# Scores of two heads by one matmul: pooled keys spread into zero-padded pairs, in a kernel of attention and two mixtures of experts

## The chip, the cores and the metric

The kernel runs on one core of one Trainium2 chip. The metric is the device time of one execution in microseconds (us). An execution covers everything from the first load to the last store; several executions are timed, and one further execution is recorded by the hardware profiler.

## The reference

Three layers follow one another. Only the first is touched by the change.

```python
# layer 1: q, k, v are (4, 8, 576, 64) float32; B=4 sequences, H=8 heads, S=576, D=64
k_p = k.reshape(B, H, Sp, pool, D).mean(axis=3)      # pool = 8, so Sp = 72 pooled keys
v_p = v.reshape(B, H, Sp, pool, D).mean(axis=3)
scores = scale * np.matmul(q, k_p.transpose(0, 1, 3, 2))
attn = softmax(scores)
x = np.matmul(attn, v_p)                              # rows become (2304, 512)
# layer 2: (2304, 512) -> 1536 -> 512
gate = 1 / (1 + np.exp(-(x @ w_gate)))
x = gate * (x @ w_val) @ w_out
# layer 3: 8 experts, every token to all of them, weights P from 8 rounds of row/column scaling
out = sum(P[:, e:e+1] * (np.maximum(x @ w1[e], 0) @ w2[e]) for e in range(8))
```

## The kernel before, in words

The 2304 tokens are cut into six blocks (`j` = 0 to 5) of 384, each of three tiles (`t`) of 128 tokens. Precision is kept by splitting operands into a high and a low part and running three passes of matmuls (`mm`, L225, and `x2_step`, L549). Layer 3 comes last and takes from about 570 us to the end; it isn't touched.

Layers 1 and 2 run interleaved. Layer 2 is a list of 72 steps, one per block and per slice `f` of the hidden width: a gate product G and a value product V (12 matmuls of 384 columns each, both recorded at L225, tile `gv`) and an output product X (12 matmuls at L549, tile `big`). For the first 36 steps the blocks 0, 1 and 2 take turns, so that a slice's weights serve two blocks. A slice that is met for the first time is made from raw 64-bit words: a load, a scaling (L152 or L154), five VectorE operations (L161, L162, L171, L174, L177), a high part by ScalarE (L195) and a low part by VectorE (L199), which is the last thing the product waits for. The slice is then stored (`store_words`) and later loaded again (`load_words`). I number these made weights m0, m1, ... in the order G, V, X of slice 0, then of slice 1 and so on; m10 is the V weight of slice 3, used in step 5.

Attention for a block is a chain of small pieces. `load_q` brings a tile with 64 x 2 partitions: partitions 0 to 63 hold the even heads, 64 to 127 the odd ones. `pool_k` sums groups of eight keys on VectorE into `kp` in the same two halves. `scores` (L341) fills a PSUM bank for one tile and one half `g`: four matmuls, each with 64 rows (one head's 64 dimensions), 128 weight columns (tokens) and 72 moving columns (pooled keys). A float32 matmul appears in the trace as two instructions, so a group of `scores` is 8. Then `maxima` (VectorE, L366 and L367), `exps` (ScalarE, L373, blocks 0 to 2) or `softmax` (blocks 3 to 5), `divide`, `turn` (TensorE transposes, L402), `keep_a` (ScalarE copy, L407), `values` (L416), `x_high` (ScalarE, L428) and `x_low` (VectorE, L432). For the first two sequences the values are pooled by TensorE (`spread_v`, L319, five pieces) and kept by ScalarE (`keep_v`, L328); otherwise by `pool_v` on VectorE.

The order in which every engine gets its work is set when the program is built. `Plan.run` takes tasks with keys (due times), costs and needs (`room`: free buffers), and hands each engine the first task by key whose needs are met by its own clock. On the chip every engine then executes its list strictly in that order, and each instruction waits for its semaphores. SyncE issues all the loads and stores of this part in one list. The table `FETCH` gives the keys of the first loads; `LEAD`, `START` and `V_LATE` say how far ahead of its block attention is planned. From step 60 on, the order is written out in plain code.

Of the kernel before, what the change touches and what calls it, by code (L numbers as in the profile page):

```python
# [10 lines left out]
F32 = mybir.dt.float32  # L11
# [10 lines left out]
def attention_moe_moe_kernel(  # L22
# [217 lines left out]
    class Attention:  # L240

        def __init__(self, at, spread):
            self.at, self.spread = at, spread
            for name in ("kp", "vp", "qs", "krs", "vrs", "es", "dens", "turned", "mx", "pt"):
                setattr(self, name, {})
# [25 lines left out]
        def pool_k(self, b, hp):  # L271
            if b not in self.kp:
                self.kp[b] = self.at.tile([128, HP, SP], F32, tag="kp", name="kp", bufs=2)
            nc.vector.tensor_reduce(
                out=self.kp[b][:, hp],
                in_=self.krs.pop((b, hp)).rearrange("p (s j) -> p s j", j=POOL),
                axis=AX.X,
                op=ALU.add,
            )

        def spread_k(self, b, c, tag):
            if c == 0:
                self.pt["k", b] = bank(*tag)
                self.kp[b] = self.at.tile([128, HP, SP], F32, tag="kp", name="kp", bufs=2)
            pt = self.pt["k", b][:, : HP * SP].rearrange("p (i s) -> p i s", i=HP)
# [49 lines left out]
        def scores(self, j, t, g, tag):  # L335
            pt = bank(*tag)
            sc = self.pt["s", j, t, g] = pt[:, 0 : 4 * SP].rearrange("p (h s) -> p h s", h=4)
            pr = slice(64 * g, 64 * g + 64)
# [70 lines left out]
        def values(self, j, t, tag):  # L409
# [410 lines left out]
    with tc.manual_schedule():  # L820
# [8 lines left out]
        for base_, step_ in ((512, -8), (-505, 8)):  # L829
# [11 lines left out]
            {  # L841
                "at": 2, "big": 4, "gv": 2, "wide": NWIDE, "made": NMADE, "wa": NWA, "kr": 4, "vr": 4,
                "q": 4, "e": 2, "a": 2, "xs": 3, "h": 3, "g": 2, "kp": 2, "vp": 2,
            }
# [29 lines left out]
        def took():  # L874
# [7 lines left out]
            ("k", 0): -39.0,  # L882
            ("q", 0): -38.5,
            ("v", 0): -25.0,
            ("w", 1): -21.0,
            ("w", 2): -17.0,
            ("k", 1): -8.5,
            ("q", 1): -7.5,
            ("v", 1): -6.5,
        }  # L890
        OFF = {"g": 0.0, "v": 0.5, "o": 1.0}
        wide_of = {}
# [30 lines left out]
        def pool(b, key, step):  # L923
# [20 lines left out]
            else:  # L944
                ks = [
                    add(FETCH.get(("k", b), key - 3) + 0.01 * i, "SP", 0.45, partial(A.load_k, b, i), room=[("kr", 1)], size=0.295, step=step)
                    for i in range(HP)
                ]
                pk = [
                    add(  # L950
                        key + 0.01 * i, "DVE", 0.72, partial(A.pool_k, b, i), [ks[i]],
                        room=[("kp", 1)] if i == 0 else None, frees=[("kr", 1)], step=step,
                    )
                    for i in range(HP)
                ]
            key += V_LATE
# [20 lines left out]
            else:  # L977
                vs = [
                    add(FETCH.get(("v", b), key - 3) + 0.01 * i, "SP", 0.55, partial(A.load_v, b, i), room=[("vr", 1)], size=0.295, step=step)
                    for i in range(4)  # L980
                ]
                pvs = [
                    add(
                        key + 0.01 * i, "DVE", 1.2, partial(A.pool_v, b, i), [vs[i]],
                        room=[("vp", 1)] if i == 0 else None, frees=[("vr", 1)], step=step,
                    )
                    for i in range(4)
                ]
            pooled[b] = pk, pvs

        V_LATE = 4.3
        START = -5.5
        LEAD = {0: 30.0, 1: 28.0, 2: 9.0, 3: 27.0, 4: 14.0, 5: 20.0}
        ends_in = [((b + 1) * S - 1) // TB for b in range(B)]

        def attend(j):
# [4 lines left out]
            if j == 1:  # L1001
                lo, lead = START, n - 1.0 - START
            step = lo - 1
# [10 lines left out]
            ms = []  # L1014
            es = []
            for t in range(TPB):
                qt = add(FETCH.get(("q", j), at_key(0.0) - 2) + 0.1 * t, "SP", 0.45, partial(A.load_q, j, t), room=[("q", 1)], size=0.262, step=step)
                for g in range(2):
                    key = at_key(0.1 + 0.12 * t + 0.06 * g)
                    s = add(  # L1020
                        key, "PE", (1.0, 0.55), with_bank(("s", j, t, g), partial(A.scores, j, t, g)), kps + [qt],
                        cond=free_tag, frees=[("q", 1)] if g else (), step=step,
                    )
                    first = (t, g) == (0, 0)
                    m = add(
                        key, "DVE", 0.93 if j >= DIRECT else 0.6, partial(A.maxima, j, t, g), [s],
                        room=[("e", 1)] if first else None, frees=gives(("s", j, t, g)) if j >= DIRECT else (), step=step,
                    )
                    ms.append(m)
                    if j < DIRECT:  # L1030
                        es.append(add(key, "ACT", 1.2, partial(A.exps, j, t, g), [m], table="exp",
                            frees=gives(("s", j, t, g))
                            + [("kp", 1) for b in range(B) if ends_in[b] == j and (t, g) == (TPB - 1, 1)]))
            if j >= DIRECT:
                x = add(
                    at_key(0.48), "ACT", 1.65, partial(A.softmax, j), ms, step=step, table="exp",
                    frees=[("kp", 1) for b in range(B) if ends_in[b] == j],
                )
            for t in range(TPB):
# [6 lines left out]
                for g in range(2):  # L1046
# [6 lines left out]
                        add(  # L1053
                            key, "ACT", 0.58, partial(A.keep_a, j, t, g), [r],
                            room=[("a", 1)] if g == 0 else None, frees=gives(("a", j, t, g)), step=step,
# [3 lines left out]
                vv = add(  # L1059
                    key, "PE", (1.25, 0.9), with_bank(("x", j, t), partial(A.values, j, t)), cs + vps,  # L1060
                    cond=free_tag, step=step,
                    frees=[("a", 1)] + [("vp", 1) for b in range(B) if ends_in[b] == j and t == TPB - 1],
                )
                xh = add(key, "ACT", 0.6, partial(A.x_high, j, t), [vv], room=[("xs", 1)] if t == 0 else None, step=step)
                xl = add(key, "DVE", 0.69, partial(A.x_low, j, t), [xh], frees=gives(("x", j, t)), step=step)
# [727 lines left out]
```

## Time and profile before

| | us |
|---|---|
| executions timed | 2051.07, 2058.88, 2059.80 (median 2058.88) |
| the profiled execution | 2051.49 |
| its span, first to last instruction | 2049.8 |
| first score matmul | 7.58 |
| first product of layer 2 | 43.41 |

The profile lists, for each engine, busy time and the groups of instructions, and for each stretch of the span what the engines did. PE is TensorE's matmuls, PEld its weight loads, DVE is VectorE, ACT ScalarE, POOL GpSimd, SP SyncE. A matmul's duration includes the time in the pipeline, so what one costs is read from the distance between starts, not from its duration. The granted clock of TensorE is given per stretch; before its first record the profile prints 1.00.

### The profile page before, as it was taken

The numbers are of one execution on the slowest core, as the hardware profiler recorded it, in microseconds if no ns is written. First come the engines' busy times: TensorE is split into PE (matmuls) and PEld (weight loads), VectorE is DVE, ScalarE is ACT, GpSimd is POOL, SyncE is SP. The second block draws the span as 40 slices with busy tenths as digits, with TensorE's granted clock in tenths as the row PEclk, the third lists the DMA queues.
The fourth block names the chain that finished last, engine by engine and source line by source line (L and its number), as shares of the span: only waits on it lengthen the run. The fifth ranks groups of instructions, "written<-read, shape, count | busy, mean of one in ns | idle before, by whom it ended". The sixth has DMA issues, their size and how long they took to land.

```text
span 2049.8 us, 33256 instructions
## 1 busy us (share of the span) xinstructions
PE 2021.3 (99%) x12721; PEld 1930.4 (94%) x12721; DVE 1257.1 (61%) x2302; ACT 786.3 (38%) x1611; POOL 682.5 (33%) x629
## 2 busy tenths in 40 slices
PE   8999999999989999999998999999999999999998
PEld 5999999999979888898888999999999999999998
DVE  7888754332168776666664656656565665656555
ACT  6734322322144443433334444444443333333332
POOL 0000000001144654445425566556654222222222
PEclk9999999999999999999999999999999999999999
DMA  7587588588866777667778877887789767676764
GB/s 262 202 313 278 185 296 302 193 299 288 322 244 233 282 277 257 247 244 264 257 270 327 295 279 279 291 284 269 279 284 372 274 248 251 240 257 227 263 241 159
DMA packets 171854, 544.83 MB, mean 266 GB/s; under 512 B 15984, under 2 KB 65136, under 8 KB 155312
## 3 DMA queue, kind: packets, MB, share of 16 engines
q1 hardware_dynamic: 171216, 541.14, 73.4%
q8 instruction: 100, 1.64, 0.3%
q0 software_dynamic: 480, 1.57, 0.2%
q14 instruction: 58, 0.48, 0.1%
HBM read 376.72 MB, written 165.94 MB: 265 GB/s over the span
## 4 chain that ended last, share of the span: by engine, by line
PE 93%; DMA 4%; DVE 1%; ACT 1%; issue 0%; POOL 0%; SPq 0%; DVEq 0%; ACTq 0%
PE big L1533 22%; PE at L1381 19%; PE gv L225 14%; PE gv L1381 14%; PE big L1412 12%; PE big L549 7%; PE at L341 1%; DMA b<-w2d 1%; PE at L416 1%; PE at L402 1%; DMA xf<-xd 1%; DMA vr<-in_v_dram 1%; DMA fa<-fad 1%; ACT e L373 0%; PE at L319 0%
## 5 line engine op out<-in xcount | busy, mean ns | idle before, releaser
L1472 POOL TENSOR_TENSOR s<-hs,s 128x384 fp32r<-128x384 f32 x192 | 195.2, 1017 | 410.9 <-ACT s L1475 261.6
L225 PE MATMUL gv<-xs,wa 128*128 128x384 f32 x1728 | 323.1, 338 | 0.1
L225 PEld LDWEIGHTS gv<-xs,wa 128*128 128x128 f32 x1728 | 298.6, 188 | 4.6 <-issue 2.0
L1412 PE MATMUL big<-w2hl,h 128*128 128x512 f32 x1152 | 296.9, 394 | 0.0
L1515 DVE SCALAR_TENSOR_TENSOR acc<-big,prob,acc 128x256 f32<-128x256 f32 (+1 forms) x462 | 254.5, 585 | 44.7 <-PE big L1533 44.7
L1412 PEld LDWEIGHTS big<-w2hl,h 128*128 128x128 f32 x1152 | 213.8, 188 | 34.4
L1381 PE MATMUL at<-xf,fs 128*128 128x384 f32 x1152 | 236.4, 340 | 2.0 <-ACT c L1594 0.9
L1381 PE MATMUL gv<-xf,fs 128*128 128x384 f32 x1152 | 233.3, 337 | 1.8 <-DVE a L1462 1.8
L1381 PE MATMUL at<-xf,fa 128*128 128x384 f32 x1152 | 227.9, 337 | 4.2 <-DVE gv L1602 2.1
L1381 PEld LDWEIGHTS at<-xf,fa 128*128 128x128 f32 x1152 | 198.5, 188 | 10.8 <-DVE gv L1602 2.7
L1381 PEld LDWEIGHTS gv<-xf,fs 128*128 128x128 f32 x1152 | 198.0, 189 | 7.5 <-DVE a L1462 2.1
L1381 PEld LDWEIGHTS at<-xf,fs 128*128 128x128 f32 x1152 | 196.9, 188 | 7.2 <-ACT c L1594 1.2
L589 POOL TENSOR_TENSOR fx<-x,fx 128x768 fp32r<-128x768 f32 x2 | 3.7, 1846 | 492.6 <-ACT fx L588 489.4
L1533 PE MATMUL big<-t,s 128*128 128x256 f32 x1152 | 162.7, 282 | 0.8 <-DVE acc L1515 0.8
L549 PE MATMUL big<-h,wa 128*128 128x384 f32 x864 | 162.2, 335 | 0.0
L1533 PE MATMUL big<-b,a 128*128 128x256 f32 x1152 | 159.0, 283 | 2.1 <-DVE a L1462 1.9
L1533 PEld LDWEIGHTS big<-t,s 128*128 128x128 f32 x1152 | 157.1, 189 | 1.0 <-DVE acc L1515 1.0
L1597 DVE TENSOR_TENSOR gv<-gv,c 128x384 f32<-128x384 f32 x64 | 36.3, 567 | 196.6 <-PE gv L1381 192.8
L1533 PEld LDWEIGHTS big<-b,a 128*128 128x128 f32 x1152 | 153.6, 190 | 3.0 <-DVE a L1462 2.9
L1441 DVE SCALAR_TENSOR_TENSOR acc<-big,prob,acc 128x512 f32<-128x512 f32 x144 | 107.5, 747 | 70.9 <-PE big L1412 68.8
L549 PEld LDWEIGHTS big<-h,wa 128*128 128x128 f32 x864 | 150.5, 188 | 0.3
L1475 ACT ACTIVATE s<-hs 128x384 fp32r<-128x384 f32 x192 | 100.5, 524 | 110.5 <-DVE hs L1468 110.5
(185 smaller groups left out, 3076.0 us busy)
## 6 DMA issues: line engine op xcount, KB each, us to landing
wa<-words SPq DMA_DIRECT2D x144, 512.0 KB, 5.9
fs<-fsd SPq DMA_DIRECT2D x64, 1024.0 KB, 8.2
fa<-fad SPq DMA_DIRECT2D x64, 768.0 KB, 6.3
b<-w2d SPq DMA_DIRECT2D x192, 256.0 KB, 4.1
raw<-in_moe_w_dram SPq DMA_DIRECT2D x64, 512.0 KB, 7.1
fsd<-fs SPq DMA_DIRECT2D x32, 1024.0 KB, 5.5
w2d<-w2hl SPq DMA_DIRECT2D x32, 1024.0 KB, 3.9
fad<-fa SPq DMA_DIRECT2D x32, 768.0 KB, 5.4
```

Source lines behind the costliest of these rows:

```text
L225: nc.tensor.matmul(out=out_, lhsT=a[s], rhs=b[m], start=(i == 0), stop=(i == n - 1))
L341: nc.tensor.matmul(out=sc[c0:c1, i], lhsT=self.qs[j, t][pr, i, c0:c1], rhs=self.kp[b][pr, i], start=True, stop=True,)
L402: nc.tensor.transpose(out=pa[:, i], in_=self.es[j][:, t, 4 * g + i], identity=ident)
L549: nc.tensor.matmul(out=x2p[d][:, :TB], lhsT=w[s][:, d * 128 : (d + 1) * 128], rhs=gs[j, f][m], start=(first and i == 0), stop=(last and i ...
L1381: nc.tensor.matmul(out=pt[:, :TB], lhsT=w[:, s, i, k], rhs=t[:, o, k], start=(start and m == 0), stop=(m == 5), skip_group_check=True,)
L1412: nc.tensor.matmul(out=py, lhsT=h[:, s, cs], rhs=w2hl[n][:, o, fh], start=(m == 0), stop=(m == 5))
L1441: nc.vector.scalar_tensor_tensor(out=acc[t], in0=py, scalar=pr, in1=acc[t], op0=ALU.mult, op1=ALU.add)
L1472: nc.gpsimd.tensor_tensor(out=t[:, 1], in0=x, in1=f32(t[:, 0]), op=ALU.subtract)
L1475: nc.scalar.activation(out=t[:, 0], in_=x, func=AF.Copy)
L1515: nc.vector.scalar_tensor_tensor(out=o, in0=src, scalar=pr, in1=o, op0=ALU.mult, op1=ALU.add)
L1533: nc.tensor.matmul(out=o, lhsT=hp[n0 + k, h][:, s, i * 128 : (i + 1) * 128], rhs=pieces2[n0, w][:, k, b], start=(first and m == 0), stop=( ...
L1597: nc.vector.tensor_tensor(out=vc, in0=vc, in1=c2, op=ALU.add)
```

## The change

Two tiles `kd` of 128 partitions x 4 pairs x 2 x 72 columns are filled with zeros once by GpSimd. After `pool_k`, two ScalarE copies (`spread_kp`) write the lower 64 partitions of `kp` to the first 72 columns of each pair and the upper 64 to the second 72. A matmul of `scores` now takes all 128 partitions of q (two heads) as weights and 144 columns of `kd`; the zeros keep the heads apart, and two matmuls fill the bank that four filled. Heads come out in natural order, which `values` follows. `kp` has one buffer, `kd` two, the ring for v three in place of four. The planner's tasks, costs and keys change with it, so the order on every engine does too.

```diff
         def __init__(self, at, spread):
+            self.kd = [at.tile([128, HP, 2, SP], F32, name=f"kd{i}") for i in range(2)]
+            for t in self.kd:
+                nc.gpsimd.memset(t, 0.0)
...
-            t = self.vrs[b, i] = self.at.tile([128, 2 * DM], F32, tag="vr", name="vr", bufs=4)
+            t = self.vrs[b, i] = self.at.tile([128, 2 * DM], F32, tag="vr", name="vr", bufs=3)
...
+        def spread_kp(self, b, g):
+            pr = slice(64 * g, 64 * g + 64)
+            nc.scalar.copy(out=self.kd[b % 2][pr, :, g], in_=self.kp[b][pr])
...
         def scores(self, j, t, g, tag):
             pt = bank(*tag)
...
             for c0, c1, b in self.pieces(j, t):
-                for i in range(4):
+                for i in range(2):
                     nc.tensor.matmul(
-                        out=sc[c0:c1, i],
-                        lhsT=self.qs[j, t][pr, i, c0:c1],
-                        rhs=self.kp[b][pr, i],
+                        out=pt[c0:c1, 2 * i * SP : 2 * (i + 1) * SP],
+                        lhsT=self.qs[j, t][:, 2 * g + i, c0:c1],
+                        rhs=self.kd[b % 2][:, 2 * g + i].rearrange("p a s -> p (a s)"),
...
-                        rhs=a[:, 4 * (h % 2) + h // 2, c0:c1],
+                        rhs=a[:, h, c0:c1],
...
         FETCH = {
             ("w", 0): -31.0,
             ("k", 0): -39.0,
-            ("q", 0): -38.5,
-            ("v", 0): -25.0,
+            ("q", 0): -35.5,
+            ("v", 0): -31.0,
...
+            kds = []
+            for g in range(2):
+                kds.append(
                     add(
+                        key - V_LATE + 0.03, "ACT", 0.42, partial(A.spread_kp, b, g), pk + kds,
+                        room=[("kd", 1)] if g == 0 else None, frees=[("kp", 1)] if g else (), step=step,
+                    )
+                )
+            pk = kds
...
-        V_LATE = 4.3
-        START = -5.5
-        LEAD = {0: 30.0, 1: 28.0, 2: 9.0, 3: 27.0, 4: 14.0, 5: 20.0}
+        V_LATE = 3.3
+        SC = 0.52
+        START = -4.5
+        END = 1.5
+        LEAD = {0: 30.0, 1: 28.0, 2: 9.0, 3: 29.0, 4: 14.0, 5: 17.0}
...
-                        key, "PE", (1.0, 0.55), with_bank(("s", j, t, g), partial(A.scores, j, t, g)), kps + [qt],
+                        key, "PE", SC * len(A.pieces(j, t)), with_bank(("s", j, t, g), partial(A.scores, j, t, g)), kps + [qt],
```

Three places show what moves. The first is the start of TensorE's list, where the scores of block 0 (L341 before, L347 now) and the pooling of v (L319, now L326) take turns; L402 is a transpose. Before:

```order
L341 MATMUL at<-kp,qt 128x72 x8
L341 MATMUL big<-kp,qt 128x72 x12
L319 MATMUL at<-vr,spread 72x512
L341 MATMUL at<-kp,qt 128x72 x4
L319 MATMUL at<-vr,spread 72x512
L402 MATMUL big<-ident,e 72x128 x4
L319 MATMUL at<-vr,spread 72x512
```

And now (L408 is the transpose):

```order
L347 MATMUL at<-kd_261,qt 128x144 x4
L347 MATMUL big<-kd_261,qt 128x144 x4
L326 MATMUL big<-vr,spread 72x512
L347 MATMUL big<-kd_261,qt 128x144 x2
L326 MATMUL big<-vr,spread 72x512
L347 MATMUL at<-kd_261,qt 128x144 x2
L326 MATMUL big<-vr,spread 72x512 x3
L408 MATMUL at<-ident,e 72x128 x4
```

The whole pooling of v stands ahead of the first transpose; before, the transposes came between its pieces.

The second place is the start of ScalarE's list: L307 is `spread_kp`, L379 the exponentials, L335 `keep_v`, L413 `keep_a`, L195 the high part of a made weight. Before (L373 the exponentials, L407 `keep_a`):

```order
L373 ACTIVATE e,den<-at,mx 128x72 x8
L373 ACTIVATE e,den<-big,mx 128x72 x12
L373 ACTIVATE e,den<-at,mx 128x72 x4
L407 COPY a<-big 72x512 x2
L195 ACTIVATE wa<-made 128x512
```

And now:

```order
L307 COPY kd_261<-kp 64x4x72 x2
L379 ACTIVATE e,den<-at,mx 128x72 x8
L379 ACTIVATE e,den<-big,mx 128x72 x12
L335 COPY vp<-big 72x512
L379 ACTIVATE e,den<-at,mx 128x72 x4
L413 COPY a<-at 72x512
```

The copies come ahead of everything, and `keep_v` stands ahead of the last exponentials of block 0.

The third place is VectorE's list up to m10, the V weight of step 5 (the last L199 of each piece). Before:

```order
L199 TENSOR_TENSOR wa<-made,wa 128x512
L171 TENSOR_SCALAR wide<-made 128x512
L174 SCALAR_TENSOR_TENSOR wide<-wide 128x512
L177 TENSOR_TENSOR made<-wide,made 128x512
L161 TENSOR_SCALAR made<-wide 128x512
L162 SCALAR_TENSOR_TENSOR made<-wide,made 128x512
L432 SCALAR_TENSOR_TENSOR xs_1166<-at,xs_1165 128x4x128
L199 TENSOR_TENSOR wa<-made,wa 128x512
```

And now, from m9 on:

```order
L199 TENSOR_TENSOR wa<-made,wa 128x512
L161 TENSOR_SCALAR made<-wide 128x512
L162 SCALAR_TENSOR_TENSOR made<-wide,made 128x512
L161 TENSOR_SCALAR made<-wide 128x512
L162 SCALAR_TENSOR_TENSOR made<-wide,made 128x512
L171 TENSOR_SCALAR wide<-made 128x512
L174 SCALAR_TENSOR_TENSOR wide<-wide 128x512
L177 TENSOR_TENSOR made<-wide,made 128x512
L171 TENSOR_SCALAR wide<-made 128x512
L174 SCALAR_TENSOR_TENSOR wide<-wide 128x512
L177 TENSOR_TENSOR made<-wide,made 128x512
L199 TENSOR_TENSOR wa<-made,wa 128x512
```

One more weight's L171, L174 and L177 stand ahead of m10, and the `x_low` (L432) that stood there has moved behind it.

## Rows read from the trace of the kernel before

**Rows 1.** The page: the chain that ended last, share of the span by engine.
```profile
PE 93%; DMA 4%; DVE 1%; ACT 1%; issue 0%; POOL 0%; SPq 0%; DVEq 0%; ACTq 0%
```

**Rows 2.** Stretches: length, then busy us by engine, PEclk, DMA share, GB/s.
```profile
21.90:43.41 21.51, 20.43 (x174) 13.81 (x172) 19.48 (x46) 18.51 (x75) 0.00 (x0) 1.00 0.51 170
93.32:134.16 40.84, 40.84 (x250) 40.04 (x250) 35.59 (x64) 17.51 (x33) 0.00 (x0) 1.00 1.00 360
134.16:524.12 389.96, 389.82 (x2405) 373.65 (x2405) 206.64 (x379) 118.21 (x203) 6.51 (x6) 1.00 0.75 265
```

**Rows 3.** Stretches of the score matmuls alone (L341, PE).
```profile
43.41:100.00 56.59, 5.54 (x40) 1.00 0.59 210
100.00:410.00 310.00, 19.77 (x160) 1.00 0.74 262
```

**Rows 4.** Timeline of PE, 124 to 135: start, us, engine, line, out<-in, count.
```profile
124.59 4.33 PE L225 MATMUL gv<-xs,wa 128*128 128x384 f32 x24
128.84 1.11 PE L341 MATMUL at<-kp,qt 64*128 64x72 f32 x8
129.88 2.35 PE L225 MATMUL gv<-xs,wa 128*128 128x384 f32 x12
132.08 2.24 PE L549 MATMUL big<-h,wa 128*128 128x384 f32 x12
134.16 2.24 PE L225 MATMUL gv<-xs,wa 128*128 128x384 f32 x12
```

**Rows 5.** Timeline of PE, 7 to 44.
```profile
7.58 2.24 PE L341 MATMUL at<-kp,qt 64*128 64x72 f32 x13 [7.58 <-DMA qt<-in_q_dram]
...
13.17 1.98 PE L319 MATMUL at<-vr,spread 128*72 128x512 f32 x2
15.08 1.98 PE L341 MATMUL at<-kp,qt 64*128 64x72 f32 x8
16.99 1.98 PE L319 MATMUL at<-vr,spread 128*72 128x512 f32 x2
...
22.05 1.02 PE L319 MATMUL at<-vr,spread 128*72 128x512 f32 x2
22.90 0.60 PE L402 MATMUL at<-ident,e 128*72 128x128 f32 x4
```

**Rows 6.** Timeline of ACT, 17 to 31.
```profile
17.86 0.32 ACT L373 ACTIVATE e<-at,mx 128x72 f32<-128x72 f32 x1 [1.36 <-DVE den L391]
...
24.59 0.57 ACT L328 COPY vp<-at 72x512 f32<-72x512 f32 x1
...
30.82 0.32 ACT L373 ACTIVATE e<-big,mx 128x72 f32<-128x72 f32 x1 [0.82 <-DVE mx L367]
```

**Rows 7.** Timeline of DVE, 6 to 91.
```profile
6.03 1.58 DVE L274 TENSOR_REDUCE kp<-kr 128x72 f32<-128x576 f32 x2 [0.81 <-DMA kr<-in_k_dram]
...
47.07 0.69 DVE L199 TENSOR_TENSOR wa<-made,wa 128x512 fp32r<-128x512 f32 x1
...
86.75 0.42 DVE L171 TENSOR_SCALAR wide<-made 128x512 uint32<-128x512 uint32 x1
...
88.55 0.42 DVE L161 TENSOR_SCALAR made<-wide 128x512 uint32<-128x512 uint32 x1
...
89.61 0.68 DVE L432 SCALAR_TENSOR_TENSOR xs<-at,xs 128x512 fp32r<-128x512 f32 x1
90.21 0.68 DVE L199 TENSOR_TENSOR wa<-made,wa 128x512 fp32r<-128x512 f32 x1
```

**Rows 8.** The stretch from m3 to m10, all engines, as rows 2.
```profile
47.80:90.90 43.10, 43.10 (x314) 40.20 (x314) 37.11 (x76) 32.51 (x84) 0.00 (x0) 1.00 0.51 180
```

**Rows 9.** Timeline of PE around step 5's V product.
```profile
90.09 1.09 PE L416 MATMUL at<-a,vp 72*64 72x128 f32 x16
91.11 6.53 PE L225 MATMUL gv<-xs,wa 128*128 128x384 f32 x36
```

**Rows 10.** Groups of DVE, 47.8 to 90.9: count, busy us, mean ns, idle before.
```profile
L366 DVE TENSOR_REDUCE mx<-at 128x4 f32<-128x288 f32 x5 | 2.3, 456 | 2.5 <-PE at L341 2.5
```

More of the change, by code (lines that the diff above doesn't have):

```diff
@@ L272, in pool_k @@
             if b not in self.kp:
-                self.kp[b] = self.at.tile([128, HP, SP], F32, tag="kp", name="kp", bufs=2)
+                self.kp[b] = self.at.tile([128, HP, SP], F32, tag="kp", name="kp", bufs=1)
             nc.vector.tensor_reduce(
@@ L283, in spread_k @@
                 self.pt["k", b] = bank(*tag)
-                self.kp[b] = self.at.tile([128, HP, SP], F32, tag="kp", name="kp", bufs=2)
+                self.kp[b] = self.at.tile([128, HP, SP], F32, tag="kp", name="kp", bufs=1)
             pt = self.pt["k", b][:, : HP * SP].rearrange("p (i s) -> p i s", i=HP)
@@ L948, in pool @@
                 ]
[L949 to L952, printed above, removed]
-                    )
-                    for i in range(HP)
-                ]
+                pk = []
+                for i in range(HP):
+                    pk.append(
+                        add(
+                            key + 0.01 * i, "DVE", 0.72, partial(A.pool_k, b, i), [ks[i], *pk[:1]],
+                            room=[("kp", 1)] if i == 0 else None, frees=[("kr", 1)], step=step,
+                        )
+                    )
             key += V_LATE
@@ L981, in pool @@
                 ]
-                pvs = [
-                    add(
-                        key + 0.01 * i, "DVE", 1.2, partial(A.pool_v, b, i), [vs[i]],
-                        room=[("vp", 1)] if i == 0 else None, frees=[("vr", 1)], step=step,
-                    )
-                    for i in range(4)
-                ]
+                pvs = []
+                for i in range(4):
+                    pvs.append(
+                        add(
+                            key + 0.01 * i, "DVE", 1.2, partial(A.pool_v, b, i), [vs[i], *pvs[:1]],
+                            room=[("vp", 1)] if i == 0 else None, frees=[("vr", 1)], step=step,
+                        )
+                    )
+            kds = []
+            for g in range(2):
+                kds.append(
+                    add(
+                        key - V_LATE + 0.03, "ACT", 0.42, partial(A.spread_kp, b, g), pk + kds,
+                        room=[("kd", 1)] if g == 0 else None, frees=[("kp", 1)] if g else (), step=step,
+                    )
+                )
+            pk = kds
             pooled[b] = pk, pvs
-        V_LATE = 4.3
-        START = -5.5
-        LEAD = {0: 30.0, 1: 28.0, 2: 9.0, 3: 27.0, 4: 14.0, 5: 20.0}
+        V_LATE = 3.3
[3 more added lines that the diff above has]
+        LEAD = {0: 30.0, 1: 28.0, 2: 9.0, 3: 29.0, 4: 14.0, 5: 17.0}
         ends_in = [((b + 1) * S - 1) // TB for b in range(B)]
@@ L1015, in attend @@
             es = []
+            xh = None
             for t in range(TPB):
@@ L1025, in attend @@
                     m = add(
-                        key, "DVE", 0.93 if j >= DIRECT else 0.6, partial(A.maxima, j, t, g), [s],
+                        key, "DVE", 0.93 if j >= DIRECT else 0.6, partial(A.maxima, j, t, g), [s, *ms[:1]],
                         room=[("e", 1)] if first else None, frees=gives(("s", j, t, g)) if j >= DIRECT else (), step=step,
@@ L1032, in attend @@
                             frees=gives(("s", j, t, g))
-                            + [("kp", 1) for b in range(B) if ends_in[b] == j and (t, g) == (TPB - 1, 1)]))
+                            + [("kd", 1) for b in range(B) if ends_in[b] == j and (t, g) == (TPB - 1, 1)]))
             if j >= DIRECT:
@@ L1036, in attend @@
                     at_key(0.48), "ACT", 1.65, partial(A.softmax, j), ms, step=step, table="exp",
-                    frees=[("kp", 1) for b in range(B) if ends_in[b] == j],
+                    frees=[("kd", 1) for b in range(B) if ends_in[b] == j],
                 )
@@ L1059, in attend @@
                 vv = add(
-                    key, "PE", (1.25, 0.9), with_bank(("x", j, t), partial(A.values, j, t)), cs + vps,
+                    key, "PE", 0.95 * len(A.pieces(j, t)), with_bank(("x", j, t), partial(A.values, j, t)), cs + vps,
                     cond=free_tag, step=step,
@@ L1063, in attend @@
                 )
-                xh = add(key, "ACT", 0.6, partial(A.x_high, j, t), [vv], room=[("xs", 1)] if t == 0 else None, step=step)
+                xh = add(key, "ACT", 0.6, partial(A.x_high, j, t), [vv, xh], room=[("xs", 1)] if t == 0 else None, step=step)
                 xl = add(key, "DVE", 0.69, partial(A.x_low, j, t), [xh], frees=gives(("x", j, t)), step=step)
```

21 lines of the change are left out of this document (10 added, 11 removed).

## The prediction

> **What bounds the kernel now.** I read the chain of waits first: TensorE holds 93% of it, so a microsecond taken from TensorE's list shortens the kernel wherever no other engine is about to become late [rows 1]. The table by stretches says where that holds. From 134 us to 524 TensorE is busy throughout, VectorE 206.64 of 389.96 us, ScalarE 118.21, and DMA is busy 0.75 of the time: there TensorE alone decides. From 93 to 134 us DMA is saturated (1.00), though TensorE still waits for nothing. Before the first product TensorE, VectorE (19.48 of 21.51) and ScalarE (18.51) are nearly full together [rows 2]. Between the first products and 91 us VectorE decides as much as TensorE: m10, the V weight of step 5, is ready at 90.21 + 0.68 = 90.89, and its product starts at 91.11 [rows 7, 9].
>
> **The score groups after 91 us.** The timeline gives a group's true price. An undisturbed product takes 132.08 to 134.16 = 2.08. From 124.59 to 134.16 stand four products and one group: 9.57 - 4 x 2.08 = 1.25 us for eight instructions. Its own rows span only 1.04 (128.84 to 129.88); the other 0.2 is lost as the engine goes from 128 rows to 64 and back [rows 4].
>
> A new group is four instructions of 128 rows, 128 weight columns and 144 moving columns; the trace has none. The nearest is the pooling piece: 128 rows, 512 moving columns, two instructions from 22.05 to 22.90, so 0.425 each or 0.83 ns a column [rows 5]. That gives 0.12 for 144 columns and 0.48 for the group, with no change of height around it. Bounds: at a product's pace (2.08 / 12 / 384 = 0.45 ns a column [rows 4]) 0.26; at what an instruction of a group costs today (1.25 / 8) 0.63. I take 0.48, from the row of the same number format and height: a saving of 0.77 (0.62 to 0.99).
>
> Between 100 and 410 us the trace has 160 of these instructions [rows 3]. 32 belong to two groups of the tile that straddles two sequences; 128 make 16 plain groups: 16 x 0.77 = 12.3 (9.9 to 15.8). A straddling group goes from 16 instructions with half the weight columns to 8 with twice the moving columns; I take 0.25 each, between 0 and 0.77. Sum after 91 us: 12.8.
>
> **The start.** Scores now wait for two copies after the last pooling, which ends at 6.03 + 1.58 = 7.61 [rows 7]. A copy of 64 x 288 lies between an exponential of 72 columns (0.32) and `keep_v` of 512 (0.57) [rows 6]; I take 0.43, the second ending 0.35 behind the first: first matmul at 8.5, 0.9 later than 7.58 [rows 5].
>
> What the early scores cost then is less of a gain than half. TensorE runs at the lower of its two levels here, 1.2 GHz: a pooling pair takes 1.91 (13.17 to 15.08) against 0.85 at 22.05, whatever the stretch prints. A lone group takes 1.91 as well (15.08 to 16.99), but the first five, 40 instructions whose halves alternate, take 7.58 to 13.17 = 5.59 [rows 5]. Five new ones take 5 x 4 x 0.24 = 4.8 at that level: 0.8 saved, where a comparison with lone groups would give 5 x 0.95 = 4.75. The Trainium skill (TensorE: Matmul & The Clock Gate, Part 3, Packing small matmuls) says that matmuls of few rows in different row groups run side by side, which speaks against merging them; by that rule the trace agrees, 0.14 an instruction in alternation against 0.24 alone. Later groups stand alone between products [rows 4], so there is no such overlap to lose.
>
> The level rose between 16.99 and 22.05, after TensorE had only full-height pooling pieces and transposes; before that, half-height scores stood among them [rows 5]. Now every score has full height from the first, so I take the rise at 13.5. Walking the new lists from there with the trace's durations: the five pooling pieces end at 18.3, `keep_v` at 19, and block 0's last exponentials, queued behind it on ScalarE, start at 19.1 instead of 17.86. But no pooling piece then stands between the transposes, and block 1's first exponentials come at 28.3 instead of 30.82 [rows 6]. From there to m3 (47.07 + 0.69 = 47.76 [rows 7]) VectorE is full, 16.9 us; its list now holds two `x_low` (0.60 each, 89.61 to 90.21) and one maxima (0.6) more: 28.3 + 16.9 + 1.8 = 47.0, with a short wait 47.5.
>
> From m3 to m10 VectorE is busy 37.11 of 43.10 us [rows 8]. The new list has three `x_low` and one maxima fewer and one narrowing more (1.80, 86.75 to 88.55 [rows 7]): 36.5. With no idle m10 is ready at 84.0, with today's 6.0 at 90.0. 2.5 of the 6.0 are waits for scores, which are shorter now and stand earlier [rows 10]; I take 2.5 idle, m10 at 86.5. TensorE would be there sooner, since three short groups replace five long ones and a values group has moved ahead; it waits for m10. So step 5's product starts 4.4 earlier (0.9 to 6.9).
>
> **Costed at nothing.** The zeroing of `kd`: GpSimd has nothing else to do until layer 3. The six later copies: ScalarE is idle two thirds of the time [rows 2]; queued before a sigmoid and made to wait for the pooling of k, each would hold up a V product by its 0.43. The third v buffer: SyncE's fourth v load of a sequence waits for VectorE to pool the first, with word loads queued behind; their cover is that words are loaded several steps ahead, and gone it costs TensorE the wait. The loads of k and q for block 3 have moved ahead of block 2's words, out of the stretch where DMA is full.
>
> **Sum.** 4.4 + 12.8 = 17.2 off the profiled execution's 2051.49: 2034.3. That execution (span 2049.8) stands 7.4 below the median; of the four executions known, two lie at 2051 and two at 2059, which the profile doesn't explain. Not knowing which level the next runs take, I add half, 3.7: 2038.
>
> **Rivals.**
>
> *The clock stays low as long as before* (20%). For it: 14 us of unbroken work did not raise it. Against: that work was half-height. Then the pooling pieces, at 1.7 each or more, end at about 22.4, block 0's last exponentials come at 23 behind `keep_v`, and m3 at 51.5; VectorE has less idle, m10 at 89.5, a gain of 1.4: 2051.5 - 14.2 + 3.7 = 2041.
>
> *A pass of 128 rows and 144 columns costs twice what I take* (12%), as if each half were still paid: 0.96 a group, saving 0.29, 16 x 0.29 = 4.6, and 2 at the start: 2048.6. Against it: the pooling piece's pace.
>
> *VectorE and TensorE wait in lock step* (8%). Place: steps 0 to 5, where weights now come just in time and VectorE's list holds work that waits for products. Price: a wait of VectorE for one product is 2.08. It decides from an idle of 84.2 + idle - 91.1 = 12.8, so 19.7 us against today's 6.0, about ten waits; with one for each of 14 products, 29 us, m10 comes at 113, 22 late: 2051.5 + 22 - 12.8 + 3.7 = 2064. For it: slack of 0.2 at m10. Against: TensorE has slack to give in exchange.
>
> **How the numbers follow.** The forecast has the remaining 60%. All low bounds together with the lower level of runs give 2051.5 - 6.9 - 15.8 = 2029; the dear pass with the upper level gives 2045 + 7.4 = 2052. Range 2029 to 2052. About 0.5%, 10.3 us, is what a measurement of this kernel can tell from no change. Faster by more: nearly all of the forecast (0.56), three quarters of the low clock (0.15), a little of the dear pass (0.02): 0.73. Slower by more: over half of the lock step, 0.05. The rest, 0.22, is within.
>
> **What would show it.** A group of scores between products should add 0.48 to 0.5, with products at 2.08; at 0.9 the dear pass is right. In the first 25 us the pooling pieces' spacing tells the clock: 0.43 from about 13.5, or 0.85 until 20. m3 should be ready near 47.5 and m10 near 86.5, TensorE waiting for VectorE just before it; if m10 comes after 91, the start has lost. Block 3's first product should come about 4.4 earlier plus what its own scores save. I am wrong if TensorE shows waits past 100 us, above all for words behind a v load, or if layer 3's length moves.

## The result, and the profile after

| | before | after |
|---|---|---|
| median of the executions timed together, us | 2059.34 (2051.07 to 2062.29) | 2033.22 (2032.29 to 2034.05) |
| ratio, with its 95% interval | | 0.9885 (0.9861 to 0.9909) |
| the profiled execution, us | 2051.49 | 2033.05 |
| first score matmul, us | 7.58 | 9.20 |
| 1st, 13th, 25th product into `gv` | 43.41, 93.32, 134.16 | 42.95, 86.37, 126.94 |
| 133rd product into `gv` (step 66) | 524.12 | 504.50 |

The change is faster, by 18.4 us between the two profiled executions and by 26.1 between the medians. The 26.1 is high: in the three later rounds the medians of the kernel before were 2056.23, 2056.39 and 2055.75 (37 executions), and the kernel after, again, took 0.9899 (0.9886 to 0.9912) of the last. Two executions, 2462.66 us (before, idle matmuls first) and 2803.69 us (half height in blocks 0 and 1), ran at a mean granted clock of 0.75 and 0.656 and are left out of the medians and ratios below. 2038 (2029 to 2052) was predicted; 2033.22 lies inside, 4.8 below the figure. I count products into `gv`, as their order differs by one place (below); the same products lie before each of the numbers. So 6.95 us are won by the 13th product, 7.2 by the 25th, 19.6 by the 133rd; layer 3 gives 1.2 back.

The groups of scores between products, TensorE's timeline after, answer to [rows 4]:

```profile
118.13 4.32 PE L225 MATMUL gv<-xs,wa 128*128 128x384 f32 x24
122.29 0.65 PE L347 MATMUL at<-kd,qt 128*128 128x144 f32 x4
122.68 2.34 PE L225 MATMUL gv<-xs,wa 128*128 128x384 f32 x12
124.86 2.24 PE L555 MATMUL big<-h,wa 128*128 128x384 f32 x12
```

The next product starts at 126.94, and 126.94 - 118.13 - 4 x 2.08 = 0.49 us for a group, where it was 1.25. In the two stretches of [rows 3] half as many instructions now take about half to three fifths of the time (length, then TensorE's busy us, its weight loads', clock, DMA share, GB/s):

```profile
43.41:100.00 56.59, 2.68 (x16) 2.36 (x16) 1.00 0.73 253
100.00:410.00 310.00, 11.97 (x80) 10.54 (x80) 1.00 0.76 270
```

From 86 us on TensorE still waits for nothing, by the table of stretches that answers to [rows 2]:

```profile
86.37:126.94 40.57, 40.57 (x249) 40.09 (x249) 36.17 (x64) 17.11 (x33) 0.00 (x0) 1.00 1.00 353
126.94:504.50 377.56, 377.56 (x2324) 365.76 (x2324) 207.10 (x381) 120.52 (x207) 6.52 (x6) 1.00 0.77 274
```

The start, TensorE's timeline after (answers to [rows 5]):

```profile
9.20 2.26 PE L347 MATMUL at<-kd,qt 128*128 128x144 f32 x8 [9.20 <-ACT kd L307]
11.25 2.12 PE L347 MATMUL big<-kd,qt 128*128 128x144 f32 x8
13.17 1.51 PE L326 MATMUL big<-vr,spread 128*72 128x512 f32 x2
14.52 0.66 PE L347 MATMUL big<-kd,qt 128*128 128x144 f32 x4
15.01 1.02 PE L326 MATMUL big<-vr,spread 128*72 128x512 f32 x2
15.87 0.65 PE L347 MATMUL at<-kd,qt 128*128 128x144 f32 x4
```

The first four groups take 13.17 - 9.20 = 3.97, 0.25 a matmul instruction; the piece at 13.17 takes 1.35 and the one at 15.01 takes 0.86: the clock rose between, at 14.2 by its record, 5.0 us after the first matmul. Before it rose at 21.9, 14.3 us after the first matmul.

ScalarE and VectorE (answers to [rows 6] and [rows 7]): the copies, `keep_v`, the last exponentials of block 0, the first of block 1; then m3 and m10.

```profile
8.23 0.87 ACT L307 COPY kd<-kp 64x288 f32<-64x288 f32 x2 [5.93 <-DVE kp L277]
19.28 0.59 ACT L335 COPY vp<-big 72x512 f32<-72x512 f32 x1 [1.83 <-PE big L326]
19.77 0.32 ACT L379 ACTIVATE e<-at,mx 128x72 f32<-128x72 f32 x1
29.13 0.32 ACT L379 ACTIVATE e<-at,mx 128x72 f32<-128x72 f32 x1
```

```profile
47.80 0.68 DVE L199 TENSOR_TENSOR wa<-made,wa 128x512 fp32r<-128x512 f32 x1
85.58 0.68 DVE L199 TENSOR_TENSOR wa<-made,wa 128x512 fp32r<-128x512 f32 x1
```

m3 is ready at 48.48 and m10 at 86.26. TensorE around them (answers to [rows 9]):

```profile
83.15 1.10 PE L422 MATMUL at<-a,vp 72*64 72x128 f32 x16
84.18 6.51 PE L225 MATMUL gv<-xs,wa 128*128 128x384 f32 x36
```

The same three products as before, 6.93 us earlier, in another order. By the weights that they use in the two programs' lists they were G of step 6 (m6), V of step 5 (m10) and V of step 6 (m7); now V of step 5 comes third. So step 5's V product is not the one at 91.11 in [rows 9], as the prediction has it, but the next, at 93.32: 2.4 after m10 was ready at 90.89. Now it is the 14th product, at 88.45, 2.2 after m10. In neither kernel did TensorE wait for m10. (Where the expectations speak of step 6's first product they give the time of the 13th product; step 6's first is the 12th.)

TensorE's groups from 0 to the 25th product show what the start is made of (count, busy us, mean ns, idle before; the durations overlap, so they add up to more than the stretch). Before:

```profile
L341 PE MATMUL at<-kp,qt 64*128 64x72 f32 (+1 forms) x112 | 14.2, 296 | 7.6 <-DMA qt<-in_q_dram 7.6
L319 PE MATMUL at<-vr,spread 128*72 128x512 f32 (+1 forms) x20 | 13.2, 747 | 0.0
L341 PE MATMUL big<-kp,qt 64*128 64x72 f32 x56 | 7.7, 342 | 0.0
```

After:

```profile
L326 PE MATMUL big<-vr,spread 128*72 128x512 f32 (+1 forms) x20 | 10.6, 624 | 0.0
L347 PE MATMUL at<-kd,qt 128*128 128x144 f32 (+1 forms) x52 | 9.1, 317 | 10.2 <-ACT kd L307 9.2 <-DVE xs L438 1.0
L347 PE MATMUL big<-kd,qt 128*128 128x144 f32 (+1 forms) x36 | 6.1, 324 | 0.0
L408 PE MATMUL big<-ident,e 128*72 128x128 f32 x24 | 3.7, 275 | 1.4 <-ACT a L413 1.4
```

Scores fall from 21.9 to 15.2 and pooling pieces from 13.2 to 10.6. All in all TensorE is busy for 11.6 us less (125.50 to 113.87) and idle for 4.4 more (8.66 to 13.07): 7.2.

### The profile page after: what moved, and what is told of

Same layout as the page of the kernel before. It is cut to its first block, busy times and chain, and to the rows that moved or that the text cites. A ratio compares the mean times of both kernels' runs of the same rounds, so it can differ in the third digit from the quotient of the medians.

```text
span 2031.3 us, 32946 instructions
## 1 busy us (share of the span) xinstructions
PE 1997.5 (98%) x12561; PEld 1915.6 (94%) x12561; DVE 1256.7 (62%) x2302; ACT 789.0 (39%) x1619; POOL 683.5 (34%) x631
## 4 chain that ended last, share of the span: by engine, by line
PE 94%; DVE 3%; DMA 1%; ACT 1%; issue 1%; POOL 0%; SPq 0%; DVEq 0%; ACTq 0%; POOLq 0%
PE big L1553 23%; PE at L1401 19%; PE gv L225 15%; PE gv L1401 14%; PE big L1432 13%; PE big L555 7%; PE at L347 1%; PE at L422 1%; DMA b<-w2d 1%; PE at L408 1%; PE at L225 1%; DMA fa<-fad 1%; DMA kr<-in_k_dram 0%; DVE acc L1535 0%; DVE e L400 0%
## 5 line engine op out<-in xcount | busy, mean ns | idle before, releaser
L1401 PEld LDWEIGHTS at<-xf,fa 128*128 128x128 f32 x1152 | 199.7, 189 | 11.6 <-DVE gv L1622 2.5
```

Of the source, the lines that this page charges most:

```text
L1401: nc.tensor.matmul(out=pt[:, :TB], lhsT=w[:, s, i, k], rhs=t[:, o, k], start=(start and m == 0), stop=(m == 5), skip_group_check=True,)
```

## The experiments

All are the kernel after, if not said otherwise. Products are given as in the first table, from each kernel's profiled execution; rise and fall are where the trace's records of the granted clock change in the first 60 us.

| kernel | median us | profiled us | 1st, 13th, 133rd product | clock rises, falls |
|---|---|---|---|---|
| before | 2059.34 | 2051.49 | 43.4, 93.3, 524.1 | 21.9, none |
| before again | | 2051.11 | 43.4, 93.3, 523.9 | 22.1, none |
| before, idle matmuls first | 2055.32 | 2055.40 | 46.3, 96.2, 526.8 | 7.5, 24.6 to 41.6 |
| after | 2033.22 | 2033.05 | 42.95, 86.37, 504.50 | 14.2, none |
| after again | 2035.07 | 2035.28 | 45.45, 88.45, 506.56 | 13.2, 23.5 to 33.7 |
| half height in blocks 3 to 5 | 2046.65 | 2048.89 | 45.39, 88.37, 518.93 | 13.2, 23.4 to 33.7 |
| half height in blocks 0 and 1 | 2043.21 | 2046.92 | 55.2, 98.15, 516.3 | 30.6, 37.4 to 47.6 |
| half height everywhere | 2064.01 | 2064.32 | 57.6, 103.5, 534.1 | 24.4, 34.6 to 51.7 |
| halves alternate, blocks 3 to 5 | 2035.14 | 2035.69 | 42.7, 86.1, 505.9 | 13.7, none |
| order's old numbers | 2033.52 | 2032.52 | 40.9, 87.7, 506.85 | 13.9, none |
| low parts on GpSimd | 2036.59 | 2037.63 | 42.3, 88.1, 508.8 | 13.2, none |
| low parts twice | 2033.86 | 2032.97 | 42.7, 88.4, 506.9 | 13.8, none |
| idle matmuls first | 2030.94 | 2031.30 | 40.5, 83.9, 502.0 | 5.1, none |
| the same again | 2030.62 | 2030.86 | 40.3, 83.7, 502.2 | 5.4, none |

**Half height in blocks 3 to 5.** The new order, with the old matmuls where TensorE alone decides.

```diff
+                if j >= DIRECT:
+                    for i in range(4):
+                        pr = slice(64 * g, 64 * g + 64)
+                        nc.tensor.matmul(out=pt[c0:c1, i * SP : (i + 1) * SP],
+                            lhsT=self.qs[j, t][pr, i, c0:c1], rhs=self.kd[b % 2][pr, i, g], ...
```

> The changed kernel in the changed order, but in blocks 3 to 5 a group of scores is again eight... in fact four matmuls of 64 rows and 72 moving columns per head half and sequence, so eight instructions instead of four; the padded keys are still made. Theory (after 91 us the gain is the price of the matmuls and nothing else): 16 plain groups return from 0.48 to 1.25 us and two straddling ones from 0.9 to 1.2, so 16 x 0.77 + 2 x 0.31 = 12.9 us over the changed kernel, 2033.2 + 12.9 = 2046.1, with the first product of step 18 where it is in the changed kernel plus what the groups before it return, and no product before 60 us moved. Rival (the new order of the list gives the gain, and the form is worth little): 2033 to 2036.

2046.65 (2046.25 to 2048.89), against before 0.9955 (0.9942 to 0.9969). From the 13th to the 133rd product it takes 430.56, after 418.13: 12.4 more, 12.9 expected. The stretch of these matmuls has the busy time of [rows 3] to the digit:

```profile
100.00:410.00 310.00, 19.77 (x160) 17.16 (x160) 1.00 0.74 261
```

So past 91 us the form is all of the gain but 0.2 (430.79 before, 430.56 here), and the order none that shows. Its start, 2 us late, is that of the clock (see the kernel after, again).

**Half height everywhere, and in blocks 0 and 1 alone.** The same edit with no condition, and with `j < 2`.

> As the kernel with half-height scores in blocks 3 to 5, but in all six blocks: only the form of the matmuls is undone, the order, the copies into padded keys and the loads stay. Theory (the form also pays at the start): 12.9 us for blocks 3 to 5, and at the start the clock's rise later than 13.9, the four lone groups of block 2 at 0.77 each (3.1), together 16 to 20 over the changed kernel: 2049 to 2053, m10 3 to 7 us later than 85.5. Rival (the start was won by the order, not by the form): no more than the other kernel, 2046, with m10 near 86. Second rival (the clock rises at about 14 whatever the height of the scores): the pooling pieces' spacing changes from 0.85 to 0.43 at about 14 here too.

> The changed kernel in the changed order, with half-height scores in blocks 0 and 1 alone; blocks 2 to 5 keep the padded keys. Theory (what the half-height form costs at the start is above all the clock, which rises later while half-height scores stand among the pooling pieces): in all six blocks the half-height form took 17.2 us more by step 6's first product, of which block 2's four groups are 4 x 0.77 = 3.1 and the clock's fall after 34 us, which comes in some executions, up to 7; so the records show the rise at 22 to 25 us instead of 14, step 6's first product at 93 to 101 instead of 86.4, and 2040 to 2048. Rival (the loss was block 2's groups and that fall): rise before 16 us, 2033 to 2037.

2064.01 (2060.22 to 2064.37), 1.0036 (1.0024 to 1.0049) of before, and 2043.21 (2041.71 to 2046.92). Both are worse at the start than was expected of the first. With half-height scores in two blocks the pieces stay slow far past 14 us:

```profile
19.52 1.98 PE L349 MATMUL at<-kd,qt 64*128 64x72 f32 x8
21.43 5.59 PE L326 MATMUL big<-vr,spread 128*72 128x512 f32 x6
26.96 1.07 PE L419 MATMUL at<-ident,e 128*72 128x128 f32 x4
```

Three pieces take 5.53 from 21.43, 1.84 each, and the records begin at 30.6. The kernel after, run again, has a fall of the same 10 us; the 13th product stands at 98.15 against 88.45, so 9.7 us are the price of half-height scores in blocks 0 and 1 with the new order; from the first score to the 13th product TensorE spent 31.7 us at the lower level, against 14.2. Half height everywhere is 5.4 worse still. Block 2's four groups are 3.1 of it by their price between products; the level explains little more, since its fall is 6.8 longer and its rise 6.2 earlier (32.7 us at the lower level), and some 2 stay open. The rival that only block 2 and the fall count is out.

**The order's old numbers.** FETCH, OFF, V_LATE, START, END and LEAD as in the kernel before, padding as after.

> The changed kernel with the order's numbers of the kernel before (when loads are issued, how far the scores lead, when a sequence's v pooling is due): padding without the new order. Theory (matmul price): the 12.8 after 91 us stays, and of the 6.9 at the start 2 to 5 go, so 2035 to 2038. Rival (the new order gave most of it, and padding alone holds the start up by its later first matmul): 2040 to 2046, with step 5's V product after 89 us.

2033.52 (2032.52 to 2033.99), 0.9891 (0.9877 to 0.9904) of before: under both expectations. The 13th product comes at 87.7, so padding alone wins 5.65 of the 6.95, and the 133rd 2.35 later than after, so the new order is worth that much by then; layer 3 of the profiled execution, whose clock does not fall there, is 2.9 shorter and hides it. The clock rises at 13.9 here too. With the experiments above this reads: the padded form needs no new order, the new order needs the padded form.

**Halves that alternate.** In blocks 3 to 5 half-height matmuls again, but both groups of a tile together, lower and upper half in turn, each into its own bank.

```diff
+            for c0, c1, b in self.pieces(j, t):
+                for i in range(4):
+                    for x in range(2):
+                        pr = slice(64 * x, 64 * x + 64)
+                        nc.tensor.matmul(out=self.pt["s", j, t, x][c0:c1, i],
+                            lhsT=self.qs[j, t][pr, i, c0:c1], rhs=self.kd[b % 2][pr, i, x], ...
```

> The changed kernel, but in blocks 3 to 5 the scores are half-height matmuls again, and both groups of a tile are issued together, a matmul of the lower 64 rows and one of the upper 64 in turn, each half into its own bank. So 64-row work that can run side by side is side by side, which it is not where a group stands alone. Theory (what the merge saves is only that a lone half-height group leaves half of the rows idle and pays for changes of height): in the kernel with half-height scores in all blocks such alternating instructions stood 0.055 us apart at the full clock (32.58 to 32.86), so a tile takes 16 x 0.055 + 0.2 = 1.1 against 2 x 0.49 for padded keys: 8 x 0.1 = about 1 us over the changed kernel, 2033.5 to 2036. Rival (side by side does not hold between products, or the change of height costs per matmul): 2.5 a tile as with lone groups, 2045 to 2047.

2035.14 (2033.71 to 2036.04), as the first theory had it. TensorE's timeline:

```profile
107.01 2.25 PE L225 MATMUL gv<-xs,wa 128*128 128x384 f32 x12
109.18 1.11 PE L350 MATMUL at<-kd,qt 64*128 64x72 f32 x16
110.23 2.35 PE L568 MATMUL big<-h,wa 128*128 128x384 f32 x12
112.42 4.33 PE L225 MATMUL gv<-xs,wa 128*128 128x384 f32 x24
```

112.42 - 107.01 - 2 x 2.08 = 1.25 for the 16 instructions of a tile: as much as a lone group of 8 took before, and 0.27 more than two padded groups. Most of the 12.4 us is thus to be had without padding. The Trainium skill (TensorE: Matmul & The Clock Gate, Part 3, Packing small matmuls) says that matmuls in different row groups run side by side; by that rule the trace agrees, 16 in the time of 8. What the change removed was not small matmuls but small matmuls that stood alone.

**Idle matmuls first.** Before the plan, 16 matmuls of the identity into a `gv` bank that nobody reads; in after (twice) and in before.

```diff
+        wt = bank("gv", 2)
+        for _ in range(16):
+            nc.tensor.matmul(out=wt[:, :128], lhsT=ident, rhs=ident, start=True, stop=True)
```

> The changed kernel with 16 more matmuls of 128 x 128 of the identity, whose result nobody reads, put ahead of everything on TensorE, so that the clock may rise before the first scores. Theory (the start is set by scores and pooling pieces at the lower clock): scores at 0.12 instead of 0.24 a matmul, pooling pieces at 0.43 from the first, block 0's last exponentials at 17 to 18 instead of 19.8, and the end 1 to 2.5 us earlier: 2030.7 to 2032.2. Rival (VectorE's and ScalarE's own lists and the loads set the start): block 0's last exponentials within 0.7 us of 19.8, time within 0.5 us of the changed kernel's 2033.2. Second rival: the clock doesn't rise by it, nothing moves.

> The changed kernel with the 16 idle matmuls ahead, again, to be compared with the changed kernel on one chip. Theory: 2 to 2.5 us under it in every pair, 2030.4 to 2032.1. Rival (the first difference was the chip's): no difference.

> The kernel before with 16 idle matmuls of the identity ahead of everything on TensorE, the counterpart of the changed kernel with the same. Theory (what the change won at the start is mostly the earlier rise of the clock): TensorE's pooling pieces fall from 13.2 to 10.1 us and its early scores by about 4, of which waits for exponentials give some back, so step 6's first product 3 to 7 earlier than 93.3 and 2045 to 2049 us; the distance to the changed kernel with the same matmuls (2030.9) is then 12.5 for the groups after 91 us plus 1.5 to 5. Rival (the half-height scores themselves set the start, whatever the clock): within 1 us of the kernel before's quicker runs, 2051 to 2053. If the spread of the kernel before (2051 to 2058) is from the clock falling again in the first 50 us, this kernel, whose TensorE is busy sooner, shows it in its records too where it takes over 2050.

With after: 2030.94 (2030.38 to 2032.13) and 2030.62 (2029.81 to 2032.00), 0.988 (0.9866 to 0.9893) and 0.9878 (0.9866 to 0.9891) of before; beside it on the same chip the kernel after took 2034.49 to 2035.28 (ratio 0.9979, 0.9972 to 0.9987, worked out from four executions of each), with a fall of the clock that this one does not show. It is the fastest kernel here. Its scores run at 0.13 an instruction from the first, TensorE's timeline of the second:

```profile
1.43 5.72 PE L847 MATMUL gv<-ident 128*128 128x128 f32 x32 [1.43 <-POOL ident masks.py:199]
9.01 1.22 PE L347 MATMUL at<-kd,qt 128*128 128x144 f32 x8 [1.86 <-ACT kd L307]
10.06 1.14 PE L347 MATMUL big<-kd,qt 128*128 128x144 f32 x8
```

The 13th product comes 2.45 and 2.64 earlier than after, the 133rd by nearly the same. With before the expectation failed: 0.999 (0.9979 to 1.0001). The clock rose at 7.5, and fell at 24.6 for 17 us, from the stretches (columns as [rows 2]):

```profile
18.00:24.00 6.00, 5.01 (x49) 3.30 (x49) 5.90 (x13) 4.46 (x10) 0.00 (x0) 1.00 1.05 391
24.00:30.00 6.00, 6.00 (x54) 5.72 (x54) 4.91 (x14) 4.35 (x24) 0.00 (x0) 0.55 0.92 321
30.00:36.00 6.00, 6.00 (x30) 4.14 (x29) 4.16 (x12) 4.26 (x26) 0.00 (x0) 0.50 0.40 130
36.00:42.00 6.00, 6.00 (x23) 4.03 (x23) 4.28 (x10) 1.78 (x7) 0.00 (x0) 0.53 0.00 0
```

What was won until 23 us was lost there: the 13th product is 2.9 later than before. An early rise alone is worth nothing if the level isn't kept.

**Does VectorE decide steps 1 to 5?** The low parts of m4 to m11 once on GpSimd, once issued twice on VectorE.

```diff
+    ON_POOL = range(4, 12)
...
-        nc.vector.tensor_tensor(out=w[:, 1], in0=made.pop(m), in1=f32(w[:, 0]), op=ALU.subtract)
+        eng = nc.gpsimd if m in ON_POOL else nc.vector
+        eng.tensor_tensor(out=w[:, 1], in0=made.pop(m), in1=f32(w[:, 0]), op=ALU.subtract)
...
-            d = add(n, "DVE", 0.69, lambda: split_low(m), [c], frees=[("made", 1)])
+            d = add(
+                n, "POOL" if m in ON_POOL else "DVE", 1.5 if m in ON_POOL else 0.69, lambda: split_low(m), [c], frees=[("made", 1)]
+            )
```

```diff
+        t = made.pop(m)
+        for _ in range(2 if 4 <= m < 12 else 1):
+            nc.vector.tensor_tensor(out=w[:, 1], in0=t, in1=f32(w[:, 0]), op=ALU.subtract)
```

> The changed kernel with the low parts of eight weights (m4 to m11) subtracted on GpSimd, which is idle then, instead of on VectorE: 8 x 0.6 = 4.8 us less for VectorE between 48 and 86 us. Theory of the prediction (VectorE decides as much as TensorE in steps 1 to 5, so weights that come earlier start step 5 earlier): first product of step 6 up to 4 us earlier than 86.4, 2029 to 2032. Rival (TensorE has no idle time left from 44 to 86 us, its own list decides): 0 to 0.5 us, 2032.5 to 2033.5. Second rival: GpSimd is slower at it or gets in VectorE's way, and weights come late: 2034 to 2037.

> The changed kernel with the subtraction that makes the low part of a weight issued twice, to the same result, for eight weights (m4 to m11): 8 x 0.68 = 5.5 us more for VectorE between 48 and 86 us, where it idles 1.8 of 37.7. Theory of the prediction (VectorE decides there as much as TensorE): step 6's first product 3.7 to 5.5 later than 86.4, 2037 to 2039. Rival (TensorE's list decides, weights have room): under 1 us, 2033 to 2034.

On GpSimd: 2036.59 (2034.57 to 2038.39), slower, the second rival. VectorE's own operations grow beside GpSimd's (46 to 90 us, as the groups above). With GpSimd:

```profile
L162 DVE SCALAR_TENSOR_TENSOR made<-wide,made 128x512 uint32<-128x512 uint32 x9 | 7.3, 810 | 0.3
L161 DVE TENSOR_SCALAR made<-wide 128x512 uint32<-128x512 uint32 x9 | 4.9, 541 | 0.0
```

After:

```profile
L162 DVE SCALAR_TENSOR_TENSOR made<-wide,made 128x512 uint32<-128x512 uint32 x8 | 5.5, 692 | 0.3
L161 DVE TENSOR_SCALAR made<-wide 128x512 uint32<-128x512 uint32 x8 | 3.4, 420 | 0.0
```

The means hide single operations that took about 1 us longer beside a subtraction on GpSimd (one of 1.75 and one of 1.52 at these two lines); the others took what they take alone. So VectorE got little of its 5.5 us back, and each subtraction took 1.39 instead of 0.68. The Trainium skill (SBUF — State Buffer, Who interferes with whom) says that VectorE operations with two inputs in SBUF contend with a GpSimd one that reads it, and that operations of a tensor with a constant can; by that the trace agrees: of the ten operations on weights (L161 to L177) that overlapped a subtraction, five took longer. The planner's cost for the moved operations changed too, and the order with it, so not all of the 3.4 us over the kernel after need be this. Twice on VectorE: 2033.86, and the 13th product 2.06 later, between the two expectations, of 5.5 us added; layer 3 of the profiled execution, again without a fall, is 2.5 shorter and hides it. TensorE waits for VectorE twice early (0.33, which the kernel after has too, and 0.15) and at these two places:

```profile
71.66 2.01 PE L227 MATMUL gv<-xs,wa 128*128 128x384 f32 x10 [0.35 <-DVE wa L201]
80.83 2.18 PE L557 MATMUL big<-h,wa 128*128 128x384 f32 x11 [0.79 <-DVE h L1130]
```

VectorE thus has some 3 us of room before it decides: near the bound, and not the bound.

**The two kernels again.**

> The kernel before, unchanged, for its trace alone: its executions lie between 2051 and 2062 us while those of the changed kernel lie within 2. Theory: the longer ones are those in which TensorE's granted clock, after its first rise, falls to the lower level again for 10 to 17 us within the first 60 us, as in the two kernels with half-height scores; if this execution takes 2055 or more, its records show such a fall and step 6's first product comes later than 93.3 by the difference, and if it takes 2051 to 2053, they show none. Rival: the difference lies in layer 3 or in the DMA.

> The changed kernel, unchanged, beside the others on one chip. Both theories: 2032 to 2034.5, as on the first chip. If the kernel before's spread comes from the clock falling again early, the executions of this kernel should show a mean granted clock of 0.997 or more, where the kernel before reaches 0.993.

The kernel before came at 2051.11 with the trace of the first time. No trace here is of one of its long executions. But every execution has a mean clock, and 37 of them, beside the experiments, line up by it in the main: at 0.999 four, 2051.34 to 2051.87; at 0.996 nine, 2055.08 to 2058.39; at 0.993 three, 2060.66 to 2062.78. Two at 1.000 don't fit (2052.45 and 2053.57), and the five at 0.995 spread from 2054.94 to 2059.89. 0.006 of 2050 us is 12 us lost to the lower level, for 10 us more of time. Where the lower level lay in them is argued from the kernel with idle matmuls, not shown.

The kernel after, again, shows what a fall costs it, from the stretches:

```profile
14.00:22.00 8.00, 6.57 (x32) 3.51 (x31) 7.30 (x20) 6.68 (x36) 0.00 (x0) 1.00 1.04 391
22.00:28.00 6.00, 5.27 (x41) 4.03 (x41) 5.13 (x10) 3.05 (x7) 0.00 (x0) 0.62 1.05 355
28.00:34.00 6.00, 6.00 (x46) 5.36 (x42) 4.70 (x14) 5.31 (x25) 0.00 (x0) 0.52 0.32 93
```

Its execution took 2035.28, 2.2 more than the one without the fall, and 2.06 of it are there by the 133rd product. The eight executions of after span 3.0 us, those of before 11.7.

## Why the prediction was right, and where it was off

- **The late groups: right.** 0.48 us a group was predicted, 0.49 measured; products stayed at 2.08. A straddling group saves 0.31, not 0.25 (the stretches with two of them and six products take 14.92 before, 14.29 after). 12.8 in all, 12.7 between the 13th and the 133rd product, and 12.4 when undone alone. The change of height as the reason for the 0.2 beyond a group's own rows is not shown: a padded group too costs 0.49 where its rows span 0.39 (122.29 to 122.68).
- **The start: 4.4 where it was 6.9, and its last step wrong.** The dates of the walk were 18.3 for the last piece (19.2), 19.1 for block 0's last exponentials (19.77), 28.3 for block 1's first (29.13), 47.5 for m3 (48.48), 86.5 for m10 (86.26); the first matmul, at 9.20 and not 8.5, shifted them, since the last load of k came later. What failed is "it waits for m10", and with it the reading that VectorE decides as much as TensorE before 91 us. The product at 91.11 does not use m10; the one that does started 2.4 after m10 was ready, and [rows 8] has TensorE busy for 43.10 of 43.10 us. The "slack of 0.2 at m10" was 2.4. TensorE worked on while m10 was made, before and after, and the gain by then is its whole list's, 6.93, and not the date of one weight. I had seen that TensorE would be there sooner, and still booked VectorE's date. m10's own date came within 0.24 by luck, as m3's was 0.98 off; and step 5's V product came 4.87 earlier (93.32 to 88.45), near the 4.4, only because it lost a place in the list, 2.08.
- **Where the start's gain lies.** The first account had 0.8 us less for the early scores and the rest through the clock. With the fall the kernel after spends 14 us at the lower level (9.3 to 13.2 and 23.5 to 33.7), as many as before (7.6 to 21.9), and still has the 13th product 4.9 earlier. So, by estimate from these two executions, some 2.1 of the 6.95 is the level that was kept, and the rest less work for TensorE, whose idle time rose (above).
- **The clock's rise: right**, 13.5 against 14.2. In six other runs with full-height scores from the start, and nothing ahead of them, it came at 13.2 to 13.9, in four with half-height ones at 21.9 to 30.6.
- **Costed at nothing: right.** The copies take 0.43 each, as estimated, and from 86 to 504 TensorE waits for no v load.
- **The level of runs: mis-sized.** 3.7 us were added for executions at the upper level. The kernel after shows no such gap between its executions (3.0 us over eight); that part of its gain over the median (26.1 against 18.4) is the spread of before.
- **The 4.8 us** between 2038 and 2033.2 are then 2.5 from the start and 3.7 from the level, less the 1.2 that layer 3 gave back and 0.2 by which the median lies above the profiled execution. Layer 3's length, from the 133rd product to the end of the profiled time, was 1525.7 to 1530.7 in these kernels, shortest in the two whose records show no fall in it (order's old numbers, low parts twice); why it differs by 1 between executions with equal records stays open.
- **The rivals.** The clock did not stay low, the pass did not cost double, and TensorE's waits after the first product are 0.3 us: no lock step.

## What to carry to other kernels

Price a small matmul by the distance between its neighbours' starts, alone and in company: half-height work that stands alone between full-height products pays for both halves, and either merging by zeros or issuing both halves in turn gets it back. Where two engines are near-bound, walk both lists to the same piece of work, as it stands in the new order, and take the later, instead of the date of one wait; and look up in the program which weight a product uses, since two times that lie 0.2 apart are not yet a wait. At this kernel's start a few idle matmuls were worth 2 to 3 us with the padded scores, and nothing with the half-height ones, where the clock fell again.

## What was not expected of the hardware

- The same list, run twice, kept the clock once and lost it for 10 us the other time (23.5 to 33.7), and that cost 2.1 us by the 133rd product, though TensorE was busy 6.58 and 6.57 of the 8 us ahead.
- Half-height scores among the pooling pieces put off the rise from 13 or 14 us to 22 to 31, with TensorE busy without a gap from the first score to the rise.
- VectorE's operations slow from 0.42 to 0.54 and 0.69 to 0.81 us on average while GpSimd subtracts, by single ones that take about 1 us longer (0.69 becomes 1.75 once).
